# Packing attention output to 128 rows before the output projection, with a separate bias row, a longer E ring and a new tile table

## The chip, the cores and the metric

One core of one Trainium2 chip. The metric is the device time of one execution in microseconds (us). The kernel before takes 812.62 us (median of 3, 811.1 to 812.72). All runs quoted here are of state fast. A profiled span is about 2 us shorter than the device time of the same run (809.2 against 811.03 before), so spans are compared with spans and medians with medians.

Engine names in the profile: PE is TensorE, PEld its weight loads, ACT ScalarE, DVE VectorE, POOL GpSimd, SP the engine that issues most DMAs.

## The reference, cut to what matters

```python
xn  = layernorm(x)                              # x: 2048 rows of 512
q   = xn @ wq                                   # 32 heads of 16
k,v = xn @ wk, xn @ wv                          # one key/value head for all
o   = softmax(q k^T / 4) v                      # 32 heads x 2048 x 2048 scores
y   = gelu(xn @ w1 + b1) @ w2 + b2              # hidden size 1792
out = x + o.reshape(2048, 512) @ wo + y
```

## The kernel before

Query rows come in 4 blocks of 512, heads in 8 groups of 4. A score tile is 128 keys by 512 queries of one head; there are 2048. Three tiles are one unit: three score matmuls run side by side in three row strips of TensorE (32 rows by 128 columns each). Of each unit ScalarE takes three tiles, or two while VectorE takes one with a cheaper approximation of exp that needs five PV matmuls in place of one. `DTAB` says, unit by unit, which tile goes to VectorE (`0` or `2`) or none (`.`). PV, the projections and the MLP run as four matmuls of 128 rows by 32 columns side by side, one per column strip (`mm4`):

```python
def mm4(o, l, rh, start, stop, r=(), w=(), allow=1.5, **ak):
    for j in range(4):
        c = slice(32 * j, 32 * j + 32)
        add("pe", lambda e, c=c, j=j: e.matmul(o[c, :], l[:, c], rh, start=start, stop=stop,
                                               tile_position=(0, 32 * j)),
            ... occ=0.216, lat=0.23, allow=allow, kind="side", tag=(None, j), **ak)
```

Each call of `add` is one operation for a list scheduler inside the kernel program, which fixes the order on every engine when the kernel is built. Its model of TensorE knows three modes ("row" for scores, "col" for `mm4` and PV, "full") and charges `SWITCH = 0.1` for a change. The four parts of a step are independent operations, so they may be placed apart.

The output of a head group lies in PSUM in strips of 32 rows: 16 rows of output, then the sum of weights, then zeros. The output projection uses it as it lies, eight steps of `mm4` for each 128 rows of output; half of the rows multiply zeros. The bias b2 rides along in a row that is free:

```python
wop = sb([P, NGR, D], bf, "wop")                       # NGR = 8 groups, 4 x 32 rows each
dma("sp", wop[16:17, 0, :], B_b2..., "d_b2", w=["wop"]) # row 16 of the output is 1 after normalising
...
def out_tile(tb, i):
    y_mm(tb, i, al=Y_ALLOW)                            # 14 steps of the MLP
    wo_mm(tb, i, range(NGR), al=Y_ALLOW)               # 8 steps of the projection
    ti = tb * 4 + i
    dve(lambda e: e.tensor_tensor(x_sb[:, ti, :], pM, x_sb[:, ti, :], ALU.add), ...)
    store(tb, i)
```

Output tiles of a block are computed during the next block, about 240 to 320, 420 to 500 and 620 to 700 us; those of the last block from about 745 us to the end.

## Time and profile before

The prediction splits the profiled span into four parts, the ledger: the time until the first exponential starts (head), ScalarE's own work, which is the count of exponentials of each kind times their undisturbed step (0.917 us for two tiles, 1.343 us for three) plus 25.5 us of tanh, the stalls of ScalarE, which are what is left between the first and the last exponential, and the tail from the last exponential's end. The step lengths are the constant distances between ends of neighbouring exponentials in the records.

### The profile page before, as it was taken

The page shows a single profiled execution, that of the slowest core. Times are in us where ns is not written, and L with a number is a line of the kernel's source. Part 1 is how long each engine was busy: PE and PEld are TensorE (multiplying, and loading weights), DVE is VectorE, ACT ScalarE, POOL GpSimd, SP SyncE. Part 2 cuts the span into 40 slices and gives each one's busy share as a digit, 9 for nine tenths or more (in the row PEclk, how much of TensorE's full clock was granted, in tenths as well). Part 3 has the DMA queues.
Part 4 walks back from the last instruction along what each step waited for, and adds up shares of the span by engine and source line. Part 5 has one row for each costly group of instructions (what it writes and reads, how often), then busy time and mean ns, then how long its engine had stood idle before and what let it go on. Part 6 is the DMA issues. An engine that isn't in the chain of part 4 may idle for free.

```text
span 809.2 us, 21055 instructions
## 1 busy us (share of the span) xinstructions
PE 782.9 (97%) x9082; PEld 245.4 (30%) x9082; DVE 739.7 (91%) x1403; ACT 785.3 (97%) x734; POOL 23.7 (3%) x79
## 2 busy tenths in 40 slices
PE   6799999999999999999999999999999999999998
PEld 4322322222323333333232333223232232233223
DVE  7499999999999978999999978799998897999985
ACT  4899999999999999999999999999999999999995
POOL 6500000000000000000000000000000000000000
PEclk7799999999999999999999999999999999999999
DMA  9000000000000000000000000000000000000001
GB/s 307 15 23 15 17 15 15 2 16 15 15 15 22 22 22 10 15 16 15 16 3 22 22 21 22 15 10 8 16 15 16 22 22 22 9 15 16 9 9 41
DMA packets 23975, 19.08 MB, mean 24 GB/s; under 512 B 12369, under 2 KB 19402, under 8 KB 23882
## 3 DMA queue, kind: packets, MB, share of 16 engines
q1 hardware_dynamic: 22298, 17.17, 7.5%
q8 instruction: 72, 1.18, 0.6%
q10 hardware_dynamic: 1584, 0.56, 0.3%
q14 instruction: 21, 0.17, 0.1%
HBM read 14.98 MB, written 2.35 MB: 21 GB/s over the span
## 4 chain that ended last, share of the span: by engine, by line
ACT 81%; PE 17%; DMA 1%; POOL 1%; issue 0%; DVE 0%; ACTq 0%; POOLq 0%
ACT E L864 77%; PE pAll L885 7%; PE pAll L845 5%; PE pAll L560 4%; ACT ub L987 3%; DMA ub<-in_A_wq_dram 1%; PE pAll L554 1%; ACT ub L684 0%; ACT xnT L702 0%; POOL V L803 0%; PE pAll L697 0%; POOL wqp L806 0%; ACT KT L716 0%; PE pAll L1152 0%; ACTq L567 0%
## 5 line engine op out<-in xcount | busy, mean ns | idle before, releaser
L864 ACT ACTIVATE E<-pAll 128x1024 bf16<-128x1024 f32 (+1 forms) x683 | 748.2, 1358 | 2.7 <-PE pAll L845 2.3
L885 PE MATMUL pAll<-Dt,V 128*32 128x512 bf16 x2070 | 362.7, 383 | 0.3 <-DVE Dt L896 0.2
L881 DVE TENSOR_SCALAR Dt<-pAll 128x512 int16<-128x512 f32 x414 | 278.4, 683 | 33.9 <-PE pAll L845 33.0
L885 PE MATMUL pAll<-E,V 128*32 128x512 bf16 x1634 | 297.1, 389 | 1.1 <-DVE Of L909 0.9
L896 DVE TENSOR_SCALAR Dt<-Dt 128x1536 int16<-128x1536 int16 (+2 forms) x584 | 283.1, 529 | 1.0
L845 PE MATMUL pAll<-QT,KT 32*128 32x512 bf16 x2048 | 268.5, 386 | 11.6 <-ACT E L864 4.2
L845 PEld LDWEIGHTS pAll<-QT,KT 32*128 32x128 bf16 x2048 | 67.8, 91 | 289.8 <-ACT E L864 246.5
L885 PEld LDWEIGHTS pAll<-Dt,V 128*32 128x32 bf16 x2070 | 99.1, 94 | 103.3 <-issue 50.8
L560 PE MATMUL pAll<-w_sb,ub 128*32 128x512 bf16 x896 | 115.3, 382 | 0.0
L560 PE MATMUL pAll<-xnT,w_sb 128*32 128x512 bf16 x896 | 109.5, 382 | 0.2
L885 PEld LDWEIGHTS pAll<-E,V 128*32 128x32 bf16 x1634 | 70.3, 93 | 80.8 <-issue 64.8
L560 PE MATMUL pAll<-wop,oT 128*32 128x512 bf16 x512 | 87.8, 381 | 0.0
L973 DVE TENSOR_SCALAR hb<-pAll,b1T 128x512 bf16<-128x512 f32 x56 | 41.6, 742 | 1.7 <-PE pAll L560 1.5
L560 PE MATMUL pAll<-xnT,wqp 128*32 128x512 bf16 x496 | 39.6, 391 | 0.8 <-DVE QT L739 0.4
L560 PEld LDWEIGHTS pAll<-xnT,w_sb 128*32 128x32 bf16 x896 | 29.5, 95 | 21.1 <-issue 7.5
L560 PEld LDWEIGHTS pAll<-w_sb,ub 128*32 128x32 bf16 x896 | 30.8, 95 | 13.2 <-issue 5.9
L987 ACT ACTIVATE ub<-ub 128x1536 bf16<-128x1536 bf16 (+1 forms) x20 | 32.3, 1617 | 0.0
L739 DVE CAST QT<-pAll 128x512 bf16<-128x512 f32 x32 | 21.9, 684 | 10.8 <-PE pAll L560 9.3
L1152 PE MATMUL pAll<-xnT,zeros 128*32 128x512 bf16 x300 | 31.0, 383 | 0.0
L560 PEld LDWEIGHTS pAll<-wop,oT 128*32 128x32 bf16 x512 | 24.5, 95 | 6.7 <-issue 1.5
L909 DVE COPY Of<-pAll 128x512 f32<-128x512 f32 x31 | 21.2, 682 | 0.5 <-PE pAll L885 0.2
L920 DVE TENSOR_TENSOR oT<-Of,rbc 128x512 bf16<-128x512 f32 x31 | 21.1, 682 | 0.0
(113 smaller groups left out, 262.4 us busy)
## 6 DMA issues: line engine op xcount, KB each, us to landing
rbc<-rden_rows SPq DMA_DIRECT2D x124, 64.0 KB, 2.0
w_sb<-in_B_w_dram SPq DMA_DIRECT2D x2, 1792.0 KB, 12.9
x_sb<-in_A_x_dram SPq DMA_DIRECT2D x8, 256.0 KB, 6.6
out_dram<-x_sb SPq DMA_DIRECT2D x16, 128.0 KB, 1.7
QT<-mT SPq DMA_DIRECT2D x60, 2.0 KB
ub<-in_A_wq_dram ACTq DMA_DIRECT2D x1, 512.0 KB, 7.4
wop<-in_A_wo_dram SPq DMA_DIRECT2D x4, 128.0 KB, 2.8
den<-Of SPq DMA_DIRECT2D x31, 8.0 KB
```

The costliest lines, as they stand in the source:

```text
L560: add("pe", lambda e, c=c, j=j: e.matmul(o[c, :], l[:, c], rh, start=start, stop=stop, tile_position=(0, 32 * j)), r, [(k, j) for k in w] ...
L739: dve(lambda e: e.tensor_copy(QT[:, hq, :], bank(bk)), w=[B(bk)] + [(B(bk), j) for j in range(4)] + [("QT", hq)] + [("QTm", hq, j) for j i ...
L845: ins = e.matmul(o, l, rh, start=True, stop=True, tile_position=(q0, 0))
L864: exps.append(act(lambda e: e.activation(E[:, s0:s0 + na, :], bank(b0, na).rearrange("p (a n) -> p a n", a=na), ACT.Exp, scale=LN2 / 128.0 ...
L881: dve(lambda e: e.tensor_scalar(Dt[:, KZ, s, :], bank(bk), float(127 * 128) + SPL_D, SPL_MIN, ALU.add, ALU.max), w=[B(bk), ("D", s, KZ)], ...
L885: add("pe", lambda e, a, b: e.matmul(pO[32 * j:32 * j + 32, :], V1[:, v, kt, :], rhs, start=a, stop=b, tile_position=(0, 32 * j)), r=r + [ ...
L896: dve(lambda e, k=k: e.tensor_scalar(Dt[:, k, s0:s0 + n, :], Dt[:, KZ, s0:s0 + n, :], float(SPL_K[k]), None, ALU.add), r=[("D", s0 + i, KZ ...
L909: dve(lambda e: e.tensor_copy(Of[:, i, :], pO), w=["O", ("Of", i)], allow=0.0)
L920: onorm[gg] = dve(lambda e: e.tensor_tensor(oT[:, gg % NOT, :], Of[:, i, :], rbc[:, i, :], ALU.mult), r=[("Of", i)] + [("rbc", i, j) for j ...
L973: dve(lambda e: e.tensor_scalar(hb[:, ft % 6, :], pM, b1T[:, ft:ft + 1], None, ALU.add), r=["b1T"], w=M4 + [("h", ft % 6)], allow=ev)
L987: act(lambda e: e.activation(uu, uu, ACT.Tanh, scale=GELU_K), r=uk, w=uk, n=c, allow=al - 0.5, kind="tanh")
L1152: pr.filler = lambda e, j, o: e.matmul((pO if o else pM)[32 * j:32 * j + 32, :], zeros[:, 0:32], xnT[:, 0, 0:TBW], start=not o, stop=not o ...
```

## The change

Its intent: after normalising, 4 x 16 useful rows of each group are copied by DMA into half of a dense 128-row tile, so the projection has 4 steps in place of 8. No row is free for the bias then, so it becomes a step of its own over one row. The memory freed makes the E ring longer, and the tile table is fitted anew to the new order. The core of the diff (tables and set-up cut):

```diff
-NE_ND_KB = (20, 8, 3)
+NE_ND_KB = (24, 8, 3)
-FIN_G = 4
+FIN_G = 2
-DTAB = "....2.2020.202..."      # 414 tiles to VectorE
+DTAB = "....2..020..02..."      # 416 tiles to VectorE
-        wop = sb([P, NGR, D], bf, "wop")
+        wop = sb([P, NGR // 2, D], bf, "wop")
+        wol = sb([P, D], bf, "wol")
+        b2row = sb([1, D], bf, "b2row")
 ... (o_evac, behind the normalising product)
+            pp, h = divmod(gg, 2)
+            for j in range(HG):
+                r0 = 64 * h + Dh * j
+                dma("sp", oTp[r0:r0 + Dh, pp % NPR, :], oT[32 * j:32 * j + Dh, gg % NOT, :], ...)
 ...
+        def wo_mm(tb, i, ps, start=False, bk=7, al=1.5):
+            for n, p in enumerate(ps):
+                pp = tb * NGR // 2 + p
+                hs = [h for h in range(2) if 2 * pp + h < NTB * NGR - 1]
+                k = 64 * len(hs)
+                mm4(bank(bk), oTp[0:k, pp % NPR, i * P:(i + 1) * P], wop[0:k, p, :], start and n == 0, False, ...)
+
+        def b2_mm(bk=7, stop=True, al=1.5):
+            mm4(bank(bk), ones[0:1, :], b2row[0:1, :], False, stop, r=["ones", "b2row"], w=[B(bk)], allow=al)
 ...
-            wo_mm(tb, i, range(NGR), al=Y_ALLOW)
+            wo_mm(tb, i, range(NGR // 2), al=Y_ALLOW)
+            b2_mm(al=Y_ALLOW)
```

The very last group has no time to be packed: it keeps its strips and weights of its own (`wol`), and its partner's half is used over 64 rows.

More of the change, by code (lines that the diff above doesn't have):

```diff
@@ L50 @@
 TBL = 1
-DTAB = "....2.2020.202.2.2...22.202222..2022.20...2..2..20220.0.2222....2020.20.0202.0.002...2022.200...2.2000.0..220.2.2.0.202002020....002.2.22.0.2002.2...2.222002..02220.02...202.222202.02.2222....022222.202022..222...22200.00.0222.2022...2.20..22.2.2.20.20.....2020..2.22002020....20.22..020.222....0..22.0..2222.0...0220...20.00.0220.2200.22...22222.02.220.22220...2.22020.202202.022....2020.000.2200.2.0....202.2.2..220.0..2.0...0....2.0.2...22.00.....02220.2.222020.0....2.220.20...222222...2.22022.0022.2.2200....2222.22.202..2.22...2.220202.202.2202.0..2220.0000.222.220.....20.22.2200020..02....2..0...22...2.020.0....020202....2.02.20...2022.22.220.02022....22200222.2.2..202.0..."
+DTAB = "....2..020..02..22...22.202220..20.00.0...220...222200..02200...2.02.2200.00220.02...20222.20...022.0000...2002.0.2.20000.000...2020.2220.0..20020....02.222.0022020..2...202.202202.02.222.....02.222.2022.000.22...20220.00.0222.2022...2220.02..2.2.0022......022...20.202002.2......02.0.000222.00.0..22.0..222..200000......2200.02202.000.22....2220.02.220.22220...22.2020.202202.022....2022.20022.0000.0....20222.220020....220..22..0...0.0..20.00.....022.20..20222.002....20220.20...22022.....0.20202.0.222.220....2220222.00222.2.22...222.0022.00222.0.20...2.020000.222.222.......202.0200.0...02......0...022...22.200....002.202...02.02.20...2022.22..20.020222...22202200..220.2000...."
 Y_ALLOW = 8.0
@@ L453, in bass_parallel_sum__grouped_kv_mqa__dense_activation_gelu__prompt_kernel @@
     NE, ND, KB = NE_ND_KB
-    NOT = 10
+    NOT, NPR = 3, 5
     NV = 1 + len(SPL_K)
@@ L524, in bass_parallel_sum__grouped_kv_mqa__dense_activation_gelu__prompt_kernel @@
         oT = sb([P, NOT, TBW], bf, "oT")
+        oTp = sb([P, NPR, TBW], bf, "oTp")
         pAll = es.enter_context(nc.psum_tensor("pAll", [P, 8 * 512], f32))
@@ L810, in bass_parallel_sum__grouped_kv_mqa__dense_activation_gelu__prompt_kernel @@
         late = [pr.writer["ibi"]]
-        setup(lambda e: e.memset(wop[:], 0.0), w=["wop"], occ=3.0, due=24.0, after=late)
+        setup(lambda e: e.memset(wol[:], 0.0), w=["wol"], occ=0.4, due=24.0, after=late)
         setup(lambda e: e.tensor_copy(selL[:], ident[:, 16:113:32]), r=["ident"], w=["selL"], due=24.0, after=late)
+        dma("sp", wop[:], A_wo.rearrange("(g p) n -> p g n", p=P), "d_wo", w=["wop"], after=late)
         for j in range(HG):
-            dma("sp", wop[32 * j:32 * j + Dh, :, :],
-                bass.AP(A_wo.tensor, A_wo.offset + j * Dh * D, [[D, Dh], [HG * Dh * D, NGR], [1, D]]),
-                f"d_wo{j}", w=["wop"])
-        dma("sp", wop[16:17, 0, :], B_b2.rearrange("(o n) -> o n", o=1), "d_b2", w=["wop"])
+            dma("sp", wol[32 * j:32 * j + Dh, :], A_wo[(H - HG + j) * Dh:(H - HG + j + 1) * Dh, :], f"d_wl{j}", w=["wol"])
+        dma("sp", b2row[:], B_b2.rearrange("(o n) -> o n", o=1), "d_b2", w=["b2row"])
         TPG = HG * NT
@@ L921, in o_evac @@
                             r=[("Of", i)] + [("rbc", i, j) for j in range(HG)], w=[("oT", gg % NOT)], allow=3.0)
+            pp, h = divmod(gg, 2)
+            for j in range(HG):
+                r0 = 64 * h + Dh * j
+                dma("sp", oTp[r0:r0 + Dh, pp % NPR, :], oT[32 * j:32 * j + Dh, gg % NOT, :], f"d_op{gg % NOT}{j}",
+                    r=[("oT", gg % NOT)], w=[("oTp", pp % NPR, h, j)])
         def o_norm_last(gg):
@@ L994, in y_mm @@
                    r=[("u", ft), "w2"], w=[B(bk)], allow=al)
-        def wo_mm(tb, i, gs, start=False, stop=True, bk=7, al=1.5):
-            for n, g in enumerate(gs):
-                assert tb * NGR + g in onorm
-                mm4(bank(bk), oT[:, (tb * NGR + g) % NOT, i * P:(i + 1) * P], wop[:, g, :], start and n == 0,
-                   stop and n == len(gs) - 1, r=[("oT", (tb * NGR + g) % NOT), "wop"], w=[B(bk)], allow=al)
+        def wo_mm(tb, i, ps, start=False, bk=7, al=1.5):
+            for n, p in enumerate(ps):
+                pp = tb * NGR // 2 + p
+                hs = [h for h in range(2) if 2 * pp + h < NTB * NGR - 1]
+                assert all(2 * pp + h in onorm for h in hs)
+                k = 64 * len(hs)
+                mm4(bank(bk), oTp[0:k, pp % NPR, i * P:(i + 1) * P], wop[0:k, p, :], start and n == 0, False,
+                   r=[("oTp", pp % NPR, h, j) for h in hs for j in range(HG)] + ["wop"], w=[B(bk)], allow=al)
+        def b2_mm(bk=7, stop=True, al=1.5):
+            mm4(bank(bk), ones[0:1, :], b2row[0:1, :], False, stop, r=["ones", "b2row"], w=[B(bk)], allow=al)
         def store(tb, i):
@@ L1017, in y_tile @@
             y_mm(tb, i, al=YT_ALLOW[i])
-            wo_mm(tb, i, range(FIN_G), stop=i < 3, al=YT_ALLOW[i])
+            wo_mm(tb, i, range(FIN_G), al=YT_ALLOW[i])
+            b2_mm(stop=i < 3, al=YT_ALLOW[i])
             if i < 3:
@@ L1133, in bass_parallel_sum__grouped_kv_mqa__dense_activation_gelu__prompt_kernel @@
         for i in range(4):
-            wo_mm(tb, i, range(FIN_G, NGR - 1), start=i < 3, stop=False, bk=FB[i], al=WF_ALLOW)
+            wo_mm(tb, i, range(FIN_G, NGR // 2), start=i < 3, bk=FB[i], al=WF_ALLOW)
         for i in range(4):
-            mm4(bank(FB[i]), oT[:, (NTB * NGR - 1) % NOT, i * P:(i + 1) * P], wop[:, NGR - 1, :], False, True,
-               r=[("oT", (NTB * NGR - 1) % NOT) if i < 2 else ("oTl", 1), "wop"], w=[B(FB[i])], due=0.0)
+            mm4(bank(FB[i]), oT[:, (NTB * NGR - 1) % NOT, i * P:(i + 1) * P], wol[:, :], False, True,
+               r=[("oT", (NTB * NGR - 1) % NOT) if i < 2 else ("oTl", 1), "wol"], w=[B(FB[i])], due=0.0)
         for i in (0, 1, 3, 2):
```

## The prediction

> **What bounds the kernel now.** Read first: busy time by engine, then the chain that ended last, then what ScalarE (ACT) waited for, then its busy time stage by stage. From the page of the kernel before:
>
> ```profile
> PE 782.9 (97%) x9082; PEld 245.4 (30%) x9082; DVE 739.7 (91%) x1403; ACT 785.3 (97%) x734; POOL 23.7 (3%) x79
> ...
> ACT 81%; PE 17%; DMA 1%; POOL 1%; issue 0%; DVE 0%; ACTq 0%; POOLq 0%
> ...
> L864 ACT ACTIVATE E<-pAll 128x1024 bf16<-128x1024 f32 (+1 forms) x683 | 748.2, 1358 | 2.7 <-PE pAll L845 2.3
> ```
>
> Three engines look full, so busy shares do not decide. The chain does: 81% of the span is ACT, nearly all of it the 683 exponentials (L864), and they had 2.7 us of recorded idle ahead of them. The list of waits says who waits for whom:
>
> ```profile
> PEld pAll L845 <- ACT E L864: 246.5, 581, 1.9
> DVE Dt L881 <- PE pAll L845: 33.0, 43, 3.3
> ACT E L864 <- PE pAll L845: 2.3, 4, 0.9
> ```
>
> TensorE (PE) waits for ACT 581 times before the score matmuls (L845); ACT waits for PE four times. PE is the one with room, its 97% notwithstanding. By stage (columns: window, its length, then busy us of PE, PEld, DVE, ACT, POOL):
>
> ```profile
> 40.00:240.00 200.00, 195.57 (x2203) 58.24 (x2200) 196.26 (x375) 199.86 (x187) 0.00 (x0) 1.00 0.06 15
> 240.00:320.00 80.00, 79.42 (x1002) 24.59 (x999) 69.70 (x131) 79.77 (x75) 0.00 (x0) 1.00 0.08 19
> 320.00:420.00 100.00, 97.63 (x1060) 29.88 (x1054) 99.64 (x188) 99.03 (x92) 0.00 (x0) 1.00 0.05 13
> 420.00:500.00 80.00, 79.83 (x1022) 24.63 (x1019) 69.81 (x135) 79.43 (x75) 0.00 (x0) 1.00 0.08 22
> ```
>
> ACT is full in every stage, also where PE has most to do (240 to 320 and 420 to 500, the output projections). Its price list comes from the single records: from one exponential's end to the next is 0.917 us for two tiles (1024 elements) and 1.343 us for three, both constant within 2 ns from the 10th to the 90th percentile. A tanh over 1536 or 1024 elements takes 1.362 or 0.936. With 415 two-tile and 268 three-tile exponentials and 16 and 4 tanh: 380.6 + 359.9 + 21.8 + 3.7 = 766.0 us of pure ACT work. The first exponential starts at 30.3 and the last ends at 799.5: 769.2 us. So all stalls of ACT together are 3.2 us; single ones of 0.2 to 1.0 us lie at 36 to 47, 256, 331 to 333 and 448. Span = 30.3 head + 766.0 ACT work + 3.2 stalls + 9.7 tail = 809.2.
>
> The tail is PE and output:
>
> ```profile
> 803.67 2.49 PE pAll L560 x39
> 806.16 0.02 issue
> 806.19 0.60 ACT x_sb L1145
> ```
>
> **What the Trainium skill says.** (1) "ScalarE: Activation LUTs", section "What ACT_TABLE_LOAD costs": an ACTIVATE with immediate scale and bias takes 186 ns plus 0.833 ns per element, and neighbours overlap by about 93 ns. That gives 0.946 and 1.373 us per step; the trace has 0.917 and 1.343, the same slope and 30 ns less, and the trace is used. So a tile taken from ACT is worth 1.343 - 0.917 = 0.426 us. (2) "TensorE: Matmul & The Clock Gate", section "Why this matters for your kernels": a matmul over 32 rows takes as long as one over 128. The trace agrees: the wop group, half of whose rows are zero, takes 381 ns each, the fully used w_sb,ub group 382. Packing therefore does cut steps in half. (3) "DMA: Bandwidth & Descriptors", section "Anatomy of one DMA": about 2.0 us fixed per transfer, told for another issue path; the trace has 2.0 us for rbc and 1.4 for rden_rows, so it holds roughly here. (4) "TensorEngine Tiling (Array Packing)", "Key Properties": changing the tiling mode drains TensorE. The trace shows 0.32 us from a score matmul to the next column-tiled one against 0.22 between rounds of one mode, so some 0.1 us per switch.
>
> **The change part by part.**
> - Output projection. Before: 8 steps of 4 column matmuls for each of 16 row tiles, 512 in all (the wop group). After: 4 packed steps and a bias step, 20 per tile, and for the last block one more step for the last group (24): 12 x 20 + 4 x 24 = 336. That is 176 fewer. Four run side by side and a round starts every 0.22 us (16 matmuls from 758.41 took 1.05 us, less the 0.38 of the last: three steps of 0.22), so 176 / 4 x 0.22 = 9.7 us less PE work, almost all of it beside saturated ACT. Worth to the end: nothing directly.
> - Costs on PE. The packed operands arrive by DMA on separate semaphores, eight per pair. PE's extra semaphore waits cost 0.051 us each in the trace; at most 16 pairs x 8 x 0.051 = 6.5 us. The bias step over one row and the last pair over 64 may each switch the tiling mode: 20 steps x 2 x 0.1 = 4 us. So PE's net gain may be anywhere from 9.7 us to nothing. Also off the path.
> - Packing DMAs. 31 groups x 4 = 124 more, on SP, which now issues 282 in 131 us. At 0.46 each, 57 us more; SP has room. They delay a group: four issues (about 2 us) and one landing (about 2 us), some 4 us from the oT product to use. It matters where the last group of a block is wanted at once: that product came at 235.9 us and the first output tile's wop matmuls ran from 236.8 to 244.6, so the delay lies within the time that stage took anyway, if the static order puts other PE work there.
> - E ring of 20 to 24 tiles. The trace has no wait of an exponential for a PV matmul to give back an E slot; its only releaser is L845. Worth nothing measurable.
> - Tile table. Counting characters: 414 tiles go to VectorE (DVE) before, 416 after (179 first and 237 third tiles in place of 148 and 266). Per block of query rows 104, 105, 104, 103 in place of 104, 106, 102, 102. ACT loses two tiles: 2 x 0.426 = 0.85 us, on the path. DVE gains 2 x 0.683 and four follow-ups of 0.420 (batches: 128 of three, 13 of two, 6 of one; 12 of two before): 3.1 us, against 69 us of idle. PE gains 8 matmuls, 0.4 us.
> - Set-up. The 3.5 us memset of wop on GpSimd shrinks. It runs behind the copies that release the first scores, so the head stays 30.3.
> - Tail. The last block's output tiles lose 8 of 32 matmuls each. Behind 799.5 us some 20 of these (5 rounds, 1.1 us) leave a PE that runs without a gap from 803.67 to 806.16. But DVE's three final additions run from 804.13 to 806.27 in any case; only ACT's addition at 806.19 and its store come earlier. I take half: 0.5 us.
> - Stalls of ACT. 3.2 us now. Those at 256 and 448 (about 1.0 us) lie in output-projection stages, which PE's relief should help; the rest depends on the new order. I take 1.0 us off.
>
> Sum: 812.62 - 0.85 - 0.5 - 1.0 = 810.3 us.
>
> **The rivals.**
> 1. Packing latency reaches ACT. If PE, which works in order, stands before a packed operand for 4 us at the three block starts, scores run dry after the two units ahead (about 2.3 us) and ACT loses some 1.7 us each, 5 in all, and 1 to 2 more in the tail: about 816. For it: four issues in series and single-group handover. Against: the same kind of chain (den, rden_rows, rbc) already lives in this schedule with slack; the den reciprocal starts 6 to 7 us after issue though its packets had finished 1.5 us after it.
> 2. Mode switches and semaphore waits eat PE's saving. Then neither stalls nor tail improve: 812.62 - 0.85 = 811.8.
> 3. PE's saving is time. If PE's 97% meant a bound, 9.7 us would go: 803. Against it stand the 581 waits of PE for ACT, and the 766.0 us of ACT work between a head and tail that hardly move. To reach it some 20 more tiles would have to leave ACT, and the table moves two.
> 4. The new table bunches DVE tiles (runs without one grow from 5 units to 7; more first tiles): DVE at 91% falls behind somewhere, its score banks come free late, and ACT waits. 1 to 4 us more: 812 to 815.
>
> **Range and chances.** The floor is hard: head 30.3 + ACT work 765.2 + tail at least 8.7 is 804.2, plus the 3.4 us by which the timed median exceeds the profiled span: 807.6 with no stall at all. Upward, rivals 1 and 4 add a few us, and runs scatter by about 1.6 (811.1 to 812.72). So 810.3, range 808.0 to 813.8. Faster by over 2% needs under 796.4, below the floor: 0.02, for a misread ACT price. Slower by over 2% needs over 828.9, a stall of 16 us at least: 0.025. Within 2%: 0.955.
>
> **What would show it.** Right: 417 two-tile and 266 three-tile exponentials at the same 0.917 and 1.343 us; ACT still first in the chain at about 80%; PE's waits for ACT before L845 at or above 246 us; 336 wop and bias matmuls; ACT stalls of 1 to 4 us; last exponential near 797 to 799. Wrong: waits of PE or of L560 on the packing DMAs with ACT idle behind them (rival 1), ACT idle before L864 released by score matmuls that themselves waited for DVE (rival 4), or a last exponential before 795, which would mean that ACT's work was not the bound.

## The result, and the profile after

821.5 us (median of 4, 820.79 to 823.72), against 812.67 before. The ratio is 1.0118, 95% interval 1.0095 to 1.0141: slower clear of the noise, though by less than 2%, and outside the predicted range of 808.0 to 813.8. (A ratio is the mean time of one kernel's fast runs over that of the other's of the same rounds, so not quite the ratio of the medians.)

The page of the changed kernel, busy time, chain and the exponentials:

```profile
PE 790.3 (96%) x8946; PEld 246.8 (30%) x8946; DVE 742.3 (91%) x1409; ACT 788.0 (96%) x734; POOL 20.8 (3%) x79
...
ACT 62%; PE 35%; DMA 1%; POOL 1%; DVE 0%; issue 0%; ACTq 0%; POOLq 0%
...
L866 ACT ACTIVATE E<-pAll 128x1024 bf16<-128x1024 f32 (+1 forms) x683 | 750.5, 1324 | 9.5 <-PE pAll L847 8.6
```

Busy shares hardly moved. The chain did: PE has 35% of it in place of 17%, ACT 62% in place of 81%. ACT's recorded idle before its exponentials rose from 2.7 to 9.5 us, released by the score matmuls. By stage (window, length, busy us of PE, PEld, DVE, ACT), the three stages with output tiles:

```profile
240.00:320.00 80.00, 79.28 (x964) 23.99 (x960) 68.73 (x129) 78.60 (x73) 0.00 (x0) 1.00 0.08 21
420.00:500.00 80.00, 79.89 (x951) 23.56 (x943) 70.21 (x135) 77.45 (x74) 0.00 (x0) 1.00 0.09 25
620.00:700.00 80.00, 79.90 (x957) 24.14 (x955) 66.80 (x126) 77.61 (x72) 0.00 (x0) 1.00 0.09 25
```

PE executed fewer matmuls than before in the same windows (964 against 1002), and yet ACT is no longer full there: it lacks 1.4, 2.6 and 2.4 us. The first two of these windows in the kernel before, shown in the prediction, had 79.8 and 79.4. The ledger, from the profiled runs:

| kernel | first exp. | ACT work | stalls | tail | span |
|---|---|---|---|---|---|
| before | 30.3 | 766.0 | 3.2 | 9.7 | 809.2 |
| changed | 29.6 | 765.2 | 13.8 | 11.4 | 819.9 |

So the span grew by 10.7: 10.6 more of stalls and 1.7 more of tail, less 0.8 of ACT work (as predicted) and 0.7 of head. In the list of waits, two lines grew, first the kernel before, then the changed one:

```profile
PEld pAll L560 <- issue: 21.2, 93, 0.4
...
PEld pAll L845 <- issue: 8.2, 27, 0.5
```

```profile
PEld pAll L563 <- issue: 41.2, 151, 0.8
...
PEld pAll L847 <- issue: 29.2, 85, 0.8
```

"issue" is a gap for which the profile shows nothing awaited. Weight loads of `mm4` steps and of scores have 41 us more of such gaps. Part of that is only another name: the gaps before scores that are put down to ACT fell at the same time from 246.5 to 220.9 us. The instructions that touch the bias tile say where (the changed kernel; under "its engine sat idle" stand the cause, us and times):

```profile
L563 PE MATMUL pAll<-b2row,ones x64: 384/384/385, 241.4 to 804.7; 1*32 1x512 bf16 x64
...
its engine sat idle before it (us, times) until:
  issue: 15.6, 46
```

The order in time on PE around one of the larger stalls (start, us, line, form in rows*columns; ACT's exponential at 274.9 came 0.81 us late):

```profile
273.29 0.59 PE L887 MATMUL pAll<-Dt,V 128*32 128x512 bf16 x4
273.51 0.38 PE L563 MATMUL pAll<-wop,oTp 128*32 128x512 bf16 x1
273.82 0.38 PE L563 MATMUL pAll<-b2row,ones 1*32 1x512 bf16 x1
274.13 0.40 PE L887 MATMUL pAll<-Dt,V 128*32 128x512 bf16 x3
274.46 0.39 PE L847 MATMUL pAll<-QT,KT 32*128 32x512 bf16 x3
274.78 0.40 PE L887 MATMUL pAll<-E,V 128*32 128x512 bf16 x3
274.79 0.39 PE L887 MATMUL pAll<-Dt,V 128*32 128x512 bf16 x1
275.11 0.39 PE L563 MATMUL pAll<-b2row,ones 1*32 1x512 bf16 x1
275.43 0.39 PE L847 MATMUL pAll<-QT,KT 32*128 32x512 bf16 x3
```

Four column matmuls of 128 rows start together. The single one-row matmul starts 0.31 us after its neighbour (273.51 to 273.82), and 0.31 us later the next starts (274.13); nothing runs beside it. The 64 bias matmuls, four to a step, stand in 46 such islands (places where one-row matmuls run by themselves), because the scheduler placed the parts of a step apart.

### The profile page after: what moved, and what is told of

It reads as the page before. It is cut to its first block, busy times and chain, and to the rows that moved or that the text cites. A ratio compares the mean times of both kernels' runs of the same rounds, so it can differ in the third digit from the quotient of the medians.

```text
span 819.9 us, 20980 instructions
## 1 busy us (share of the span) xinstructions
PE 790.3 (96%) x8946; PEld 246.8 (30%) x8946; DVE 742.3 (91%) x1409; ACT 788.0 (96%) x734; POOL 20.8 (3%) x79
## 4 chain that ended last, share of the span: by engine, by line
ACT 62%; PE 35%; DMA 1%; POOL 1%; DVE 0%; issue 0%; ACTq 0%; POOLq 0%
ACT E L866 58%; PE pAll L887 15%; PE pAll L847 10%; PE pAll L563 9%; ACT ub L994 3%; DMA ub<-in_A_wq_dram 1%; ACT ub L687 1%; PE pAll L557 1%; ACT xnT L705 0%; PE pAll L1167 0%; POOL V L806 0%; POOL wqp L809 0%; ACT KT L719 0%; PE pAll L700 0%; ACTq L570 0%
## 5 line engine op out<-in xcount | busy, mean ns | idle before, releaser
L887 PE MATMUL pAll<-E,V 128*32 128x512 bf16 x1632 | 300.9, 388 | 0.4 <-DVE Of L911 0.4
L847 PEld LDWEIGHTS pAll<-QT,KT 32*128 32x128 bf16 x2048 | 67.8, 91 | 284.8 <-ACT E L866 220.9
L563 PE MATMUL pAll<-w_sb,ub 128*32 128x512 bf16 x896 | 118.6, 382 | 0.2 <-DVE hb L980 0.2
L563 PE MATMUL pAll<-xnT,w_sb 128*32 128x512 bf16 x896 | 113.3, 382 | 0.6 <-DVE x_sb L1024 0.3
L563 PE MATMUL pAll<-wop,oTp 128*32 128x512 bf16 (+1 forms) x256 | 57.0, 390 | 0.0
L563 PEld LDWEIGHTS pAll<-xnT,w_sb 128*32 128x32 bf16 x896 | 31.2, 95 | 20.9 <-issue 5.2
L563 PEld LDWEIGHTS pAll<-w_sb,ub 128*32 128x32 bf16 x896 | 32.7, 95 | 14.0 <-issue 5.7
L1167 PE MATMUL pAll<-xnT,zeros 128*32 128x512 bf16 x332 | 35.5, 383 | 0.0
L991 DVE TENSOR_TENSOR ub<-hb 128x1536 bf16<-128x1536 bf16 (+1 forms) x20 | 18.0, 899 | 0.2
```

Source lines behind the costliest of these rows:

```text
L847: ins = e.matmul(o, l, rh, start=True, stop=True, tile_position=(q0, 0))
L887: add("pe", lambda e, a, b: e.matmul(pO[32 * j:32 * j + 32, :], V1[:, v, kt, :], rhs, start=a, stop=b, tile_position=(0, 32 * j)), r=r + [ ...
L1167: pr.filler = lambda e, j, o: e.matmul((pO if o else pM)[32 * j:32 * j + 32, :], zeros[:, 0:32], xnT[:, 0, 0:TBW], start=not o, stop=not o ...
```

## The experiments

Theory 1: a matmul of one row in the stream of 128-row matmuls changes TensorE's tiling mode, so each island pays for a change before and after it and shares no round (a round is up to four column matmuls that start together). Theory 2: the packing DMAs, or the semaphore waits for them, hold TensorE. Theory 3: the new table or the longer ring crowds TensorE and VectorE. The ledgers of all runs, with medians and ratios to the kernel before of the same rounds:

| run | median us | ratio | first exp. | ACT work | stalls | tail | span |
|---|---|---|---|---|---|---|---|
| e1 bias over 128 rows | 807.88 | 0.995 | 29.6 | 765.2 | 2.3 | 10.4 | 807.5 |
| e2 last pair over 128 rows | 819.64 | 1.0087 | 29.8 | 765.2 | 14.8 | 8.9 | 818.6 |
| e3 both | 807.05 | 0.9945 | 29.8 | 765.2 | 1.6 | 8.6 | 805.2 |
| e4 before, one-row bias step | 849.74 | 1.0458 | 30.3 | 763.7 | 22.8 | 31.3 | 848.1 |
| e5 before, 128-row bias step | 837.68 | 1.0314 | 29.7 | 763.7 | 10.3 | 30.8 | 834.5 |
| e8 one-row bias, four together | 810.62 | 0.9984 | 30.2 | 765.2 | 2.7 | 11.0 | 809.0 |
| e7 e3 with the old table | 819.39 | 1.0085 | 30.4 | 766.0 | 8.7 | 11.7 | 816.8 |
| e6 e3 with a ring of 20 | 810.18 | 0.9968 | 30.5 | 765.2 | 4.4 | 9.4 | 809.5 |
| e10 e3, nobody waits for packing | 810.39 | 0.9982 | 29.9 | 765.2 | 3.2 | 10.2 | 808.5 |
| e9 e3, bias added by GpSimd | 815.25 | 1.0044 | 29.8 | 765.2 | 10.3 | 8.6 | 813.9 |
| e11 e3 with a table of 420 | 804.31 | 0.9915 | 29.6 | 763.5 | 0.8 | 8.7 | 802.6 |
| e12 e9 with a table of 423 | 811.05 | 0.9988 | 30.9 | 762.2 | 8.1 | 8.7 | 809.9 |

All were correct but e10, which is wrong on purpose. In e4 and e5 two of the 20 tanh run after the last exponential, so 2.3 us less of ACT work lies between first and last (the expectation of e5 gives e4's stalls without this correction, 20.6). The profiled runs of e1, e6 and e10 each had half the clock for 3.4 us near 392 to 397 us, where each lost 1.2 us in stalls; e3's had not. So differences of a us between ledgers say little.

### e1: the bias over 128 rows

```diff
-        b2row = sb([1, D], bf, "b2row")
+        b2row = sb([P, D], bf, "b2row")           # rows 1 to 127 set to zero
-            mm4(bank(bk), ones[0:1, :], b2row[0:1, :], False, stop, ...)
+            mm4(bank(bk), ones[:], b2row[:], False, stop, ...)
```

> The changed kernel with the bias step fed from 128 rows (a bias tile with zeros below its first row, a 128-row ones tile as weights) in place of one row; the instruction order on TensorE, VectorE and ScalarE is the same, instruction for instruction. Theory 1 (the 64 one-row matmuls each change TensorE's tiling mode and stand alone, about 0.3 us before and after in place of a shared 0.22 us round): ScalarE's stalls fall from 13.8 us to 3 to 5, the tail stays at 11.4, so about 811 to 812 us. Theory 2 (packing transfers or their semaphore waits hold TensorE): no change, 821. Theory 3 (new table or ring crowd TensorE and VectorE): no change, 821.

Measured: 807.88 us, ratio 0.995 (0.993 to 0.9971). The order of instructions on PE, DVE and ACT is identical to that of the changed kernel, only the rows differ, so the 13.6 us between the medians (821.5 less 807.88) belong to the one-row matmuls. (The spans of the two profiled runs differ by 12.4 only, as e1's profiled run was the slowest of its four, 809.21 us.) Stalls fell to 2.3 us where theory 1 expected 3 to 5, the tail to 10.4 where it expected 11.4, so the time lies 3 us under the expected range; ACT is full again between 240 and 320 us. PE near the same place, the window from 240 to 320 us, and the bias tile's idle line:

```profile
272.03 0.38 PE L563 MATMUL pAll<-b2row,ones 128*32 128x512 bf16 x1
272.03 0.38 PE L888 MATMUL pAll<-Dt,V 128*32 128x512 bf16 x1
272.04 0.38 PE L563 MATMUL pAll<-wop,oTp 128*32 128x512 bf16 x1
```

```profile
240.00:320.00 80.00, 78.87 (x988) 23.53 (x982) 70.34 (x132) 80.00 (x75) 0.00 (x0) 1.00 0.08 22
```

```profile
  issue: 1.1, 5
```

The bias matmul of e1 belongs to a round of others, as 63 of the 64 do; of the 15.6 us of idle before bias matmuls 1.1 remain. Theories 2 and 3 expected 821 and fall as explanations of the loss: packing, table and ring are all still in e1.

### e2 and e3: the half-filled pair

```diff
+        wo3 = sb([P, D], bf, "wo3")               # the partner's 64 rows of weights, zeros below
-                mm4(bank(bk), oTp[0:k, ...], wop[0:k, p, :], ...)
+                mm4(bank(bk), oTp[:, ...], wop[:, p, :] if k == P else wo3[:], ...)
```

> The changed kernel with the last block's half-filled pair read over 128 rows (weights zero below row 64) in place of 64 rows; the one-row bias stays. Theory 1 (mode switches, and in the tail a TensorE clock that falls because the switches leave it idle): only the tail shortens, from 11.4 to 9.5 to 10.5 us, stalls stay at 13.8: about 820 us. Theory 2: the tail waits for the last packing transfer, which stays, so 821.5. Theory 3: 821.5.

> Both edits of e1 and e2: no matmul of the output projection uses fewer than 128 rows. Theory 1: 809.5 to 811, a little under the kernel before, as the prediction's sum without the mode switches gave. Theories 2 and 3: 820 to 821.

Measured: e2 819.64, e3 807.05. In e2 the tail fell from 11.4 to 8.9 us, somewhat more than expected, and nothing else improved; e3 came out 2.5 us under its range because the stalls are smaller than expected. The chain at the end of the changed kernel, with its clock (the column behind POOL's in the second view), and at the end of e3:

```profile
812.15 4.77 PE pAll L563 x24
```

```profile
812.00:815.00 3.00, 3.00 (x22) 0.56 (x20) 1.76 (x3) 0.00 (x0) 0.00 (x0) 0.54 0.07 20
815.00:818.00 3.00, 1.82 (x9) 0.32 (x8) 0.73 (x2) 0.60 (x1) 0.00 (x0) 0.50 0.35 116
```

```profile
799.94 0.65 PE pAll L564 x8
800.61 1.29 DVE x_sb L1161 x2
```

In the changed kernel the last 24 matmuls alternate between 64-row and 128-row steps and take 4.8 us, in part because the granted clock is half of full from 812 us on. In e2 and e3 the clock stays full until the last matmul has run. The Trainium skill, "TensorE: Matmul & The Clock Gate", section "Part 1: The HAM clock gate", says that a clock gate follows TensorE's recent activity. What sets it off here is not shown: the clock fell in the tails with 64-row steps (changed kernel, e1, e8), but also at 803.4 us in e6's, which has none. The records do show what each part costs for a round in the tail: 0.22 us in e3 (full clock, no change of rows), 0.33 in e1 before its clock fell (800.33 to 801.31, a change at every round), 0.43 in e6 (half clock, no change), 0.54 in the changed kernel (both). From its first to its last round this stretch takes 4.1 us in the changed kernel (812.08 to 816.20) and 1.1 in e3. Of the 3.0 us between them an estimate from these round times gives 1.4 to the changes and the rounds that are no longer shared, and 1.7 to the clock.

### e4 and e5: the bias step in the kernel before

e4 takes the bias out of the free row of `wop` and adds `b2_mm` over one row to each output tile of the kernel before; e5 is the same over 128 rows.

```diff
-            wo_mm(tb, i, range(NGR), al=Y_ALLOW)
+            wo_mm(tb, i, range(NGR), stop=False, al=Y_ALLOW)
+            b2_mm(al=Y_ALLOW)                      # ones[0:1], b2row[0:1] in e4; ones[:], b2row[:] in e5
```

> The kernel before, with its bias taken out of the padding row of the projection weights and added by the one-row step instead (64 more matmuls); no packing, old table, ring of 20. Theory 1: slower by 8 to 14 us, 821 to 827, stalls of ScalarE in the output-tile stages. Theories 2 and 3: 64 matmuls in 16 rounds of 0.22 us are 3.5 us of TensorE work beside ScalarE, so 812.5 to 814.

> The control of e4: the kernel before with a separate bias step, but over 128 rows. e4 was 37 us slower, more than the 8 to 14 expected, with 20.6 us of ScalarE stalls and a tail of 31 us. If the mode switches made all of that, this run is back at 812.5 to 815. If e4 also suffered from 64 more matmuls in an order and table not tuned for them (the tail points to it), this run is slow too and only the switches' share goes: e4 less the 13.6 us that e1 gained, about 834 to 838.

Measured: e4 849.74, e5 837.68. e4 missed its range by 23 us, so by itself it proves nothing; e5 is the control. Between the two lie 12.1 us of median; by the ledgers 12.5 us of stalls, against 11.5 between the changed kernel and e1: the cost of the one-row form again, without packing, with the old table and the short ring. e5 lies in the second of its two expected ranges. The other 25 us over the kernel before are not the one-row form. Both have a tail of 31 us, in which PE still works on output tiles after ACT has finished (in e5, 152 matmuls between 820 and 830 us, the last exponential having ended at 803.7). So 64 more matmuls, 3.5 us of PE work, upset the order that the old table was fitted to. Why the last block bears it was not pursued.

### e8: one-row matmuls, four together

The changed kernel; after scheduling, the four one-row matmuls of a step are moved to the place of the last of them.

```diff
         pr.schedule()
+        for gr in bgroups:                         # the four operations of one bias step
+            ... pr.ops = rest[:k] + gr[:3] + rest[k:]   # rest[k] is the last of the four
```

> The changed kernel with its one-row bias matmuls, but the four of a step emitted side by side at the place of the last of them, all else in the same order: 16 islands of one-row matmuls in place of 46. Theory 1 (each island costs about 0.31 us before and 0.31 after, 29 us of TensorE in 46 islands): about 10 us remain, so ScalarE's stalls fall from 13.8 to between 4 and 7 us: 811 to 814. If the number of one-row matmuls counts and not the number of switches: 821.

Measured: 810.62, ratio 0.9984 (0.996 to 1.0009). Idle before the bias tile's matmuls:

```profile
  issue: 5.2, 16
```

Still 64 matmuls of one row, but 16 islands in place of 46, and 10.9 us faster. The idle went 15.6, 5.2, 1.1 us with 46, 16 and 0 islands of another mode. So the number of islands sets the cost, not the number of short matmuls. An island is two things at once, changes of mode and a round that no other matmul shares, and e8 reduces both (four short matmuls share a round again), so it does not divide the cost between them. The gain is even somewhat larger than expected.

### e7 and e6: table and ring

```diff
 e7: -DTAB = (the new table)          e6: -NE_ND_KB = (24, 8, 3)
     +DTAB = (the old table)              +NE_ND_KB = (20, 8, 3)
```

> e3 (no short matmuls) with the old tile table. If the table's worth is the two tiles that it takes from ScalarE: 807.05 + 0.85, about 808. If the table is a fit to the new order, so that the old one crowds single stages: 810 to 818, with ScalarE stalls of 4 us and more.

> e3 with the E ring back at 20 tiles. The prediction called the ring worthless, as no exponential waited for an E slot: 807 to 808, stalls within 1 us of e3's 1.6. If the ring carries part of the gain: 809 or more, with waits of exponentials for PV matmuls.

Measured: e7 819.39, e6 810.18. The old table costs 12.3 us in the new order, of which 0.8 is ACT work, 7.1 stalls and 3.1 tail by the ledger; that is just above the range given for a table that is a fit to the order. A table is a fit to one order. That also says what packing and padding earn with an unfitted table: nothing, e7 is slower than the kernel before. The ring is not settled: e6's interval (0.9934 to 1.0001) overlaps e3's (0.992 to 0.9969), e6's own runs lie between 807.84 and 811.88, and its profiled run had two windows of 3.4 us at half clock that e3's had not. Its two runs with the higher mean clock (0.989 and 0.993) took 807.84 and 809.18, the two with the lower (0.981 and 0.98) 811.18 and 811.88. Up to 3 us for the ring stay open.

### e10: nobody waits for the packing

```diff
-                mm4(bank(bk), oTp[:, pp % NPR, i * P:(i + 1) * P], ...
-                   r=[("oTp", pp % NPR, h, j) for h in range(2) for j in range(HG)] + ...
+                mm4(bank(bk), xnT[:, p, i * P:(i + 1) * P], ...
+                   r=tr(0, 4) + ...                # ready from the start; wrong result on purpose
```

> e3 with the packed projection steps reading a tile that is ready from the start in place of the packed one (a wrong result on purpose): the packing transfers are still issued, but nothing on TensorE waits for them. Theory 1 (packing was hidden, only the short matmuls cost): as e3 within 1.5 us, 805.5 to 808.5. Theory 2 (packing latency still costs in e3): 804 or less.

Measured: 810.39 us. That is 3.3 us over e3, outside the range given: with other dependences the scheduler lays another order, and the profiled run had a window of 3.4 us at half clock at 393 us, where 1.2 us of stall lie. It is not under 804, so no gain from the missing waits shows, though with another order it is no clean test; e1 and e3, which keep the packing and are faster than the kernel before, speak more clearly. The changed kernel's own view of the packed tile agrees:

```profile
L570 SPq DMA_DIRECT2D oTp<-oT x124: 523/589/1534, 77.2 to 807.9; - x124
...
who waited for it (us, times):
busy tenths in 40 slices 0000000000033430000013540000003333001138
DMA to landing us min/median/max: 1.7/1.8/3.7
```

The list of who waited is empty. Four issues of 0.59 us and a landing of 1.8 us make the 4 us that the prediction worked out, and they are hidden.

### e9, e11 and e12: can both kernels be beaten by more?

e9 drops the bias matmuls; GpSimd adds b2 to the residual instead. e11 is e3 with 420 tiles on VectorE, found by a search that changed single entries of the table; e12 is e9 with such a table of 423.

```diff
+        for ti in range(NT):
+            setup(lambda e, ti=ti: e.tensor_tensor(x_sb[:, ti, :], x_sb[:, ti, :], b2row[:], ALU.add), ...)
```

> e3 with no bias matmul at all: GpSimd adds the bias to the 16 residual tiles once, early. 64 matmuls, 16 rounds of 0.22 us, 3.5 us of TensorE work, are gone. ScalarE's stalls in e3 are 1.6 us, so at most that can be gained: 805.5 to 808; if GpSimd's additions slow VectorE at 40 to 70 us, some stalls appear there.

> e3 with a table found by a search over the order that e3 has: 420 tiles on VectorE in place of 416. ScalarE's work falls by 4 x 0.426 = 1.7 us; if TensorE and VectorE still have room: 804.5 to 806. If they have none, stalls take it back: 807 and more.

> e9 with a searched table of 423 tiles on VectorE: 7 x 0.426 = 3.0 us less ScalarE work than e9, paid for by the 3.5 us of TensorE work that the bias matmuls took: 803 to 805. If VectorE is the next bound: 806 and more, with ScalarE waiting for scores that wait for VectorE.

Measured: e9 815.25, e11 804.31, e12 811.05. e9 lies 7 us above its range (its expectation had foreseen some stalls at 40 to 70 us, without a size), and e12 missed the 803 to 805 of its first reading; e11 came out 0.2 us under its range. e9's stalls lie at 40 to 60 us (8.3 of its 10.3). GpSimd's additions, and VectorE's two affected groups between 36 and 56 us, in e9 and in e3:

```profile
L824 POOL TENSOR_TENSOR x_sb<-x_sb,b2row 128x512 bf16<-128x512 bf16 x16 | 19.9, 1282 | 0.0
```

```profile
L904 DVE TENSOR_SCALAR Dt<-Dt 128x1536 int16<-128x1536 int16 x7 | 7.9, 1167 | 0.0
...
L745 DVE TENSOR_TENSOR hb<-QT 128x512 bf16<-128x512 bf16 x3 | 4.1, 1363 | 0.0
```

```profile
L902 DVE TENSOR_SCALAR Dt<-Dt 128x1536 int16<-128x1536 int16 x8 | 4.1, 550 | 0.0
...
L745 DVE TENSOR_TENSOR hb<-QT 128x512 bf16<-128x512 bf16 x5 | 2.1, 417 | 0.0
```

The same VectorE instructions take 1.17 and 1.36 us in place of 0.55 and 0.42 while GpSimd adds. The Trainium skill, "SBUF — State Buffer", section "Who interferes with whom", says that VectorE's fast modes and its instructions with two SBUF inputs can be blocked by GpSimd for a whole instruction; this agrees with it. VectorE's PSUM reads (0.68 us) did not change. That these instructions cause the stalls is read from the trace, not tested, and the clock has a part that was not separated: it was half of full from 51.8 to 58.6 us in e9 and from 49.9 to 56.8 in e12, and full there in e3. The two stalls at 47.2 and 50.4 us (3.4 us) came before it fell. Sixteen additions spread out, not in a row, may do better; that was not tried. e12 gains 4.2 us over e9 by its seven tiles, more than the 3.0 expected, and has the same damage.

e11 is the fastest: 804.31 us, ratio 0.9915 (0.9901 to 0.993) to the kernel before. Its ACT work is 1.7 us under e3's, as counted, and its stalls are 0.8 us. That is still under 2%.

## Why the prediction was wrong

**What held.** The ACT ledger: 417 and 266 exponentials at the same steps, 0.8 us less work. The head did not grow. Packing was hidden (rival 1 fell). With the two short forms padded (e3) the change gives 807.05, where the prediction's sum, which charges nothing for mode changes, said 810.3; the extra comes from smaller stalls (1.6 in place of an assumed 2.2), a tail shorter by 1.1 in place of 0.5, a head shorter by 0.5, and some 1.6 us from where the sum starts: at the timed median (812.62), while the ledger is that of a profiled run of 811.03, under all timed ones. For the same reason the "hard floor" of 807.6 was none. Its 3.4 us between median and span compares two runs, where within one run it is 1.8 (811.03 less 809.2), and e3 lies under it at the same ACT work.

**The step that failed** is this one, under "Costs on PE": "The bias step over one row and the last pair over 64 may each switch the tiling mode: 20 steps x 2 x 0.1 = 4 us. So PE's net gain may be anywhere from 9.7 us to nothing. Also off the path." The mechanism was named, but two things in the sentence were wrong. In the sum it is the term for stalls that failed: 2.2 us assumed, 13.8 measured. Of the signs that the prediction gave for being right, ACT's share of the chain (62% for about 80%), PE's waits for ACT (220.9 us for 246 and more) and the last exponential (808.5 us for 797 to 799) failed with it.

First, the size. The unit is not the step but the island: 46 of them. Counted in the records, an island holds PE for one round of its own, 46 x 0.216 = 9.9 us, and the changed kernel has 72 more mode changes than e1 (1430 against 1358), each about 0.313 us from start to start in place of 0.216, so 72 x 0.097 = 7.0 us. Had the 64 matmuls shared rounds, they would have cost 16 x 0.216 = 3.5 us. That is an estimate of 9.9 + 7.0 - 3.5 = 13.4 us of PE time. The term was put at 4. (That the two kernels' medians also lie 13.6 us apart is in part chance, since not all of PE's loss had to reach the end.) Nor could the prediction's own check have warned it: it compared the wop group with w_sb,ub, 381 with 382 ns, but both run over 128 rows, so no matmul over few rows was in that comparison, and the time of one record does not show what a change of mode costs.

Second, the place: "off the path". That rested on the reading that PE had room because it waited for ACT 581 times, 246.5 us. But 246.5 / 581 is 0.42 us for each wait, and 0.42 is also the usual gap of the weight-load lane at a change where nothing is awaited: at the 38 changes from 128-row column matmuls to a one-row matmul in the changed kernel, for which the profile names no cause, its median is 0.425 (0.227 to 0.425). Three lines of the kernel before:

```profile
795.92 0.38 PE L560 MATMUL pAll<-wop,oT 128*32 128x512 bf16 x1
796.22 0.10 PEld L845 LDWEIGHTS pAll<-QT,KT 32*128 32x128 bf16 x3 [0.42 <-ACT E L864]
796.23 0.39 PE L845 MATMUL pAll<-QT,KT 32*128 32x512 bf16 x3
```

The scores start 0.31 us after the last column matmul, which is the shortest distance of all 644 such changes between 60 and 790 us (0.311, median 0.316). The 38 changes to a one-row matmul, with nothing awaited, take the same (0.309 to 0.320). So nothing shows that PE could have been sooner, whatever ACT did; the profile only names the semaphore that came last. What exceeds 0.31 at these changes is PE's true room: 22.8 us in all, and about 2 us in the 80 us from 240 to 320. So PE was nearly as full as ACT. Of the 13.4 us, about 1 us in each of the four output stages found room. ACT's stalls grew by 11.5 us (13.8 in the changed kernel against 2.3 in e1), somewhat more than the 9.4 that this leaves; the account closes to about 2 us.

**The rivals.** Rival 2 said that mode changes and waits eat PE's saving and put the end at 811.8, as though PE could not fall below its old state; it was the right rival with a wrong ceiling. Its other half, the semaphore waits at up to 6.5 us, did not show: PE has 253 such instructions in the changed kernel against 218 before, 35 more at 0.051 us, so under 2 us. Rival 3, that PE's saving is time, was dismissed on the same misreading of the waits. It is half right: PE's room is what lets the table move tiles away from ACT, and e11 shows that four more can go once the islands are gone. Rival 4 was not the cause: e1 has the same table and few stalls.

**The tail** was to shrink by 0.5 us and grew by 1.7. Its 64-row steps, alternating with 128-row steps, were counted as matmuls only; the mode changes and the halved clock together cost about 2.5 us (e2), more than half of it the clock by the estimate above, and without them the tail is shorter than before by 1.1 (e3).

**The table** was called worth 0.85 us, its two tiles. In the new order it is worth 12.3 us (e7), since it is a fit to the order and not a number of tiles.

**Left open:** the worth of the longer ring (0 to 3 us), what sets off the fall of the clock in some tails, its part in e9's stalls, and the 31 us tails of e4 and e5.

## What to carry to other kernels

On TensorE, count changes of tile shape, not matmuls: in this kernel a one-row matmul in a stream of 128-row column matmuls cost a round of its own and up to two changes of mode, and padding its operands with zeros to 128 rows freed it of that. Before a list of waits is taken as proof of room, divide the total by the count and compare it with the gap at changes of the same kind where nothing is awaited; if they agree, the engine may be switching, not waiting, and the distances from start to start of the matmuls tell. A saving on an engine that is off the path shows only once the schedule is fitted again to use it, and an old fit in a new order can cost more than the change brings (e7).

## What the Trainium skill lacked or had wrong

- "TensorEngine Tiling (Array Packing)" says that changing the tiling mode drains TensorE, and lists 128x32, 64x32 and 32x32 as different configurations, but gives no time and does not say that a matmul over one row falls out of the 128-row mode. Here going from 128 rows by 32 columns to 1 row by 32 columns takes 0.31 us from start to start, like going to the scores' 32 by 128; two column matmul rounds of one mode lie 0.216 apart.
- "TensorE: Matmul & The Clock Gate" states that a matmul over 32 rows takes as long as one over 128. A record of one row does (0.384 us against 0.38), but the page does not warn that in a mixed stream such a matmul may stand alone: 64 of them cost 13.6 us more than the same 64 over 128 zero-padded rows (e1).
- No page read tells that the weight-load lane shows a gap at a change of mode, here usually 0.42 us from column matmuls to scores and 0.23 us back, which a wait list puts down to whichever engine signalled last (581 times, 246.5 us).
- "ScalarE: Activation LUTs": its figures, as an estimate, give 0.946 and 1.373 us for a step of 1024 and 1536 elements from PSUM; measured were 0.917 and 1.343.
- "DMA: Bandwidth & Descriptors" gives its fixed 2.0 us for another issue path and no time to landing for a copy issued from SP; here the SBUF-to-SBUF packing copies of 16 KB, issued from SP, landed in 1.7 to 3.7 us, median 1.8.
